# One order list for all steps and loads of an attention and expert kernel: loads of q, k, v and of each weight placed singly, and fillers placed for the clock

## The chip, the cores and the metric

The kernel runs on one core of one Trainium2 chip. The metric is the device time of a run in microseconds (us); a profile shows the span from the first to the last instruction, some 1.6 us less than the time of the same execution. Engines: PE is TensorE (matrix products), PEld its weight loads, DVE is VectorE, ACT is ScalarE, POOL is GpSimd, SP is SyncE. Each works through its own line of instructions in order.

## The reference

Eight batches. Each first passes an attention without softmax, then its 576 x 512 result goes through one of eight experts, picked by the mean of that result.

```python
kv  = einsum('bhsd,bhse->bhde', k, v)            # 8 batches, 8 heads, 576 x 64
out = einsum('bhsd,bhde->bhse', q, kv)
x   = out / rms(out) * g_norm                    # heads side by side: 576 x 512
e_idx = argmax(x.mean(axis=1) @ w_gate)          # one expert per batch
gate  = softmax probability of that expert
result[b] = gate * (relu(x[b] @ w1[e]) @ w2[e])  # 512 -> 1024 -> 512
```

So the expert's weights (2.1 MB as fp16, read as fp32) can only be fetched when the batch's attention is over.

## The kernel before

The whole program is a list of tokens, `ORDER`, which is emitted from left to right into the lines of the engines. `3O1` is batch 3, step O, head pair 1. Steps: T transposes q, K is k times v, O is q times kv, M the mean square, X the normalisation, G0 to G3 the gate (product, expert, power, scale), m0 to m7 the first expert layer and m8 to m16 the second, D a filler product, meant only to keep TensorE's clock up, L a load of q, k, v, W a load of the weights, Q a VectorE copy of q. R, C and P belong to batch 0 alone: R casts its first loads, C evicts its transposes, P copies its gate row and hands PSUM (where TensorE's products lie until an engine evicts them) over to the other batches. A final `x` changes the evicting engine.

```python
def load_qkv(b, parts, which=None):          # one token L: q, k and v together
    ... bufs: qt 3, kt 4, vt 4
    nc.gpsimd.dma_start(t[0:R, hs], src[b, hs]...)

def s_dl(b, mx, pg):                         # part of the gate's value, not of the choice
    ...
    nc.gpsimd.tensor_tensor(lg, base, dl, ALU.pow)     # in GpSimd's line

def s_w(b):                                  # one token W: W1 and W2 together
    ...                                      # VectorE copies an old slot, in case the
    nc.vector.tensor_copy(W[:, own, ...], W[:, ds(sv, 1), ...])   # expert is there
    nc.gpsimd.dma_start(W1[:, own, :, fs], moe_w1[ds(ev, 1), ...], cond=cond)
    nc.gpsimd.dma_start(W2[:, own], moe_w2[ds(ev, 1)]..., cond=cond)
```

Dots mark what is cut, the comments are added. `cond` skips the load when one of the two batches before used the same expert; with these data the weights of batches 1 and 7 are skipped. All these loads cast fp32 to fp16 and are issued by GpSimd, in order, between its power operations and its waits for the expert's number.

Of the kernel before, what the change touches and what calls it, by code (L numbers as in the profile page):

```python
# [16 lines left out]
ALU = mybir.AluOpType  # L17
# [4 lines left out]




ORDER = (
    "0D9 0R1 0R2 0R0 0K02 0T02 0C0 0O0 0K12 0T12 0C1 0M0 0O1 0K22 0T22 0X0 0C2 0M1 0O2 "
    "0K32 0T32 0X1 0C3 0M2 0O30 0O31 0D4 0M30 0M31 0D6 0X2 0X30 0X31 0G1 0P0 1K0 1T0 1O0 "
    "1T1x 1T2 1T3x 1O2 0m0x 1O1 0m3x 1M0 0m5x 1X0 2L0 1M2 1M1 1O3x 1X1 0m7x 1M3 0m6 1X2 "
    "0m1 0G2 1X3 0G3 0m4 1G0 0m2 1G1 0m13 0m15 2Q0 1G3 2T0x 0m14 3L0 2T3x 2T2x 0m16x 0m11 "  # L30
    "0m12x 1W0 2T1 2K0 0m9 2O0 2O1 0m10 2M0 2X0 0m8x 2O2 2O3 3Q0 1m0 2M1 1m3x 2M2 1m7 2X1 "
    "2X2 2M3 2X3 3T0x 1m1 2G0 4L0 3K0 1m5 2G1 3O0x 1m2 3M0 1m6 3T1x 2W0 1m4 3T2 3X0 2G3 "
    "1m11 3T3x 3O1 1m12x 1m15 4Q0 3M1 3O3 1m13 4T0 1m16 3M3 3O2 1m14 1m8x 3X1 5L0 4K0 3M2 "
    "1m9 3X2 3X3 3G0 4T1x 1m10x 4O0x 2m0x 2m4x 4T3x 4T2 2m1 3G1 2m3 2m7 4M0 2m2 4O1x 3W0 "
    "2m6x 4O3x 2m5x 2m13 4M1 3G3 5Q0 2m14x 4X0 5T0x 4X1 2m9 4M3 2m10 4O2 5K0 2m8x 2m15 "
    "5T3 4M2 4X2 4X3 2m16x 5O0x 2m11 2m12 4G0 5T2x 3m0x 6L0 5M0 5O2 5X0 3m6 3m7 5T1 4G1 "
    "3m2 5O1 3m1x 5M2 3m5 6Q0 3m3 5M1 3m4 4W0 3m11 7L0 4G3 6T0x 6T3x 3m12x 6T2x 3m8x 6K0 "
    "5O3 3m15 5X1 3m16x 5X2 5M3 3m13 5X3 3m14 3m9 6O0 3m10x 5G0 4m0 5G1 4m7x 6M0 6O2x "
    "4m4x 6O3x 4m3x 6X0 4m1 6M3 4m5 5G3 6M2 4m2x 6T1x 4m6 5W0 4m11 6O1x 4m9 4m12x 7Q0 6M1 "
    "4m10 4m15 7T0 6X1 7T3x 4m16 7T1x 7K0 6X2 4m8x 7T2 6X3 7O0x 4m13 4m14x 7M0 6G0 5m0x "  # L40
    "7O2x 5m4x 6G1 5m2 7X0 5m7 6W0 5m5 5m1 5m3 5m6x 7M2 7O3 5m11 7O1 5m9 6G3 5m12x 5m10 "
    "7M1 7X1 7X2 7M3 5m13 7X3 5m14x 5m15 5m16 5m8 6m0 7G0 6m1 6m3 6m4x 6m2x 7G1 6m7 6m6 "
    "7G3 6m5 6m9 6m10 6m15 6m16x 6m11 7W0 6m12 6m13 6m14 6m8x 7m0 7m7 7m2 7m5 7m3 7m4 7m1 "
    "7m6 7m9 7m10x 7m13 7m14x 7m15 7m16x 7m11 7m12 7m8x "
)


# [1 line left out]
def kernel(  # L49
# [16 lines left out]
    P = 128  # L66
# [22 lines left out]

    st = [dict() for _ in range(B)]  # L90

    def load_qkv(b, parts, which=None):
        if kvq[b] is None:
            kvq[b] = [pqkv.tile([P, H, NJ, Dh], F16, tag=n, name=n, bufs=nb)
                      for n, nb in (("qt", 3), ("kt", 4), ("vt", 4))]
        step = H // parts
        for i in (range(parts) if which is None else which):
            for t, src in zip(kvq[b], (q, k, v)):
                hs = slice(i * step, (i + 1) * step)
                nc.gpsimd.dma_start(  # L100
                    t[0:R, hs], src[b, hs].rearrange("h (p j) d -> p h (j d)", j=NJ))
# [36 lines left out]
    def psum(tag, bufs=2, nb=2):  # L138
        return psp[0].tile([P, nb, 512], F32, tag=tag, name="ps_" + tag, bufs=bufs)
# [4 lines left out]
    def warm(t, n):  # L144
        for _ in range(n):
            nc.tensor.matmul(t[:, 0, :], ones, kvb[:, 1], start=True, stop=True)  # L146


    def s_qt(b, c, x=False, w=0):
        s = st[b]  # L150
        if "qT" not in s:
            s["qT"] = att.tile([P, NP, S], F16, tag="qT", name="qT")
        p32 = psum("t", 1, 1) if first[0] else psum("a")
        warm(p32, w)
        pt = p32.bitcast(F16)
        for j in range(NJ):
            if "qr" in s:
                nc.tensor.transpose(pt[:, 0, j * R:(j + 1) * R], s["qr"][0:R, c, j],  # L158
                                    ident[0:R, 0:R])
                continue  # L160
            for i in range(2):
                nc.tensor.transpose(pt[64 * i:64 * i + 64, 0, j * R:(j + 1) * R],
                                    kvq[b][0][0:R, 2 * c + i, j, :], ident[0:R, 0:R])
        s["pt", c] = pt
        if b > 0:
            s_tc(b, c, x)
# [12 lines left out]
    def s_tc(b, c, x=False):  # L179
        copy(x, st[b]["qT"][:, c, :], st[b]["pt", c][:, 0, 0:S])  # L180

    def s_kv(b, prs, w=0):
        kt, vt = kvq[b][1:3]
        kv = kvb[:, b % 2]
        p32 = psum("kv", 1, 1) if first[0] else psum("a")
        warm(p32, w)
        pk = p32[:, 0].rearrange("p (c e) -> p c e", c=NP)
        for c in prs:
            for j in range(NJ):
                for i in range(2):  # L190
                    nc.tensor.matmul(pk[64 * i:64 * i + 64, c, 64 * i:64 * i + 64],  # L191
                                     kt[0:R, 2 * c + i, j, :], vt[0:R, 2 * c + i, j, :],
                                     start=(j == 0), stop=(j == NJ - 1))
        cs = slice(prs[0], prs[-1] + 1)
        nc.vector.tensor_copy(kv[0:64, cs, 0:64], pk[0:64, cs, 0:64])
        nc.vector.tensor_copy(kv[64:128, cs, 64:128], pk[64:128, cs, 64:128])
# [52 lines left out]
    def s_row():  # L249
        s = st[0]  # L250
        pg = psum("t", 1, 1)[0:1, 0, 0:E]
        for c in range(NP + 1):
            nc.tensor.matmul(pg, s["pl"][:, c:c + 1], wg[:, min(c, NP - 1)], start=(c == 0),
                             stop=(c == NP))
        s["pg"] = pg
        s_index(0, pg)
        s_w(0)

    def s_index(b, pg):
        n = pg.shape[0]  # L260
# [6 lines left out]
    def s_dl(b, mx, pg):  # L267
        dl = sm.tile([P, E], F32, tag="dl", name="dl")
        nc.vector.tensor_scalar(out=dl, in0=pg, scalar1=mx[:, 0:1], scalar2=None,
                                op0=ALU.subtract)  # L270
        lg = sm.tile([P, E], F32, tag="lg", name="lg")
        nc.gpsimd.tensor_tensor(lg, base, dl, ALU.pow)  # L272
        st[b]["lg"] = lg

    def s_gate2(b):
# [18 lines left out]



    def s_w(b):
        own = b % NW
        cond = None
        if b > 0:  # L300
            sv = 0
            if b > 1:
                sv = nc.vector.value_load(st[b]["src"][0:1, 0:1], min_val=0, max_val=NW - 1)
            for W in (W1, W2):
                for h in range(2):
                    n = W.shape[2] // 2
                    nc.vector.tensor_copy(  # L307
                        W[:, own, h * n:(h + 1) * n],
                        W[:, ds(sv, 1), h * n:(h + 1) * n].rearrange("p o c f -> p (o c) f"))
            for e in evs[max(0, b - 2):b]:  # L310
                c = evs[b] != e
                cond = c if cond is None else s_logical_and(cond, c)
        ev = evs[b]
        nh = {0: 4, B - 1: 2}.get(b, 1)
        for h in range(nh):
            fs = slice(h * F // nh, (h + 1) * F // nh)
            nc.gpsimd.dma_start(W1[:, own, :, fs],  # L317
                                moe_w1[ds(ev, 1), :, fs].rearrange("o (c p) f -> p (o c) f", p=P),
                                cond=cond)
        nc.gpsimd.dma_start(W2[:, own], moe_w2[ds(ev, 1)].rearrange("o (c p) d -> p (o c) d", p=P),  # L320
                            cond=cond)
        st[b]["w"] = (W1[:, own], W2[:, own])

    def s_gate3(b):
        if b == 0:
            pg = psum("a")[:, 0, 0:E]
            nc.tensor.matmul(pg, mean[0:1], st[0]["row"], start=True, stop=True)
            mx = sm.tile([P, 8], F32, tag="mx", name="mx")
            nc.vector.max(mx, pg)
            s_dl(0, mx, pg)  # L330

    def s_gate4(b):
        gs = sm.tile([P, 1], F32, tag="gs", name="gs")
# [4 lines left out]
    def m_1(b, fb, x=False):  # L338
        s = st[b]
        if fb == 0:  # L340
            s["hT"] = hp.tile([P, 8, S], F16, tag="hT", name="hT")
        w1 = s["w"][0]
        ph = psum("m")
        for c in range(4):
            for i in range(2):
# [15 lines left out]

    def m_2(b, t, fcs, x=False):
        s = st[b]
        w2 = s["w"][1]
        if fcs[0] == 0:
            s["pm2", t] = psum("m")
        po = s["pm2", t]
# [46 lines left out]
    def emit(tok):  # L414
        x = tok[-1] == "x"
        b, f, c = int(tok[0]), tok[1], tok[2:].rstrip("x")
        h = None
        if len(c) > 1 and f in "OMXKT":
            c, h = c
            h = int(h)  # L420
        c = int(c or 0)
        if f == "m":
            unit(b, c, x)
        elif f == "D":
            warm(psum("kv", 1, 1), c)
        elif f == "R":
            cast_first(c)
        elif f == "P":
# [4 lines left out]
                                                    space=bass.MemoryType.PSUM))  # L433
            first[0] = False
        elif f == "K":
            s_kv(b, [c] if b == 0 else range(NP), h or 0)
        elif f == "C":
            s_tc(b, c)
        elif f == "G":
            if (b, c) == (0, 1):  # L440
                s_row()
            else:
                (s_gate, s_gate2, s_gate3, s_gate4)[c](b)
        elif f == "Q":
            s_qr(b)
        elif f == "W":
            s_w(b)
        elif f == "L":
            load_qkv(b, 1)
        elif f == "T":  # L450
            s_qt(b, c, x, h or 0)
        elif f == "O":
            s_o(b, c, h, x)
        else:
            dict(M=s_m, X=s_x)[f](b, c, h)
# [33 lines left out]
```

## Time and profile before

| | before |
|---|---|
| time, median of 3 (then 4) runs | 208.54 us (207.93) |
| span of the profiled execution | 203.4 us |
| TensorE busy | 179.3 us, 88% |
| VectorE / ScalarE / GpSimd busy | 116.2 / 103.4 / 51.4 us |
| cast loads / outputs and first loads | 26.30 MB / 10.05 MB |
| first expert product | 29.4 us |
| first product with W1 of batch 5 | 149.19 us |

### The profile page before, as it was taken

To read this page: it belongs to the slowest core of one execution; us is meant where nothing else is said; L and a number is where in the kernel's file an instruction comes from. 1 tells how busy PE (TensorE), PEld (TensorE's weight loads), DVE (VectorE), ACT (ScalarE), POOL (GpSimd) and SP (SyncE) were. 2 spreads that over 40 slices of the span, in tenths; PEclk is the share of its full clock that TensorE was granted. 3 is DMA by queue.
4 is the path that set the end of the run, shared out by engine and by line. 5 is a ranking of instruction groups with operands and counts; after the bars stand their busy time and mean duration, and the time that the engine had idled before them with its cause. 6 is when DMAs were issued, how large, how long until landed. Compare 5 with 4: busy or idle time off the path is not lost.

```text
span 203.4 us, 4406 instructions
## 1 busy us (share of the span) xinstructions
PE 179.3 (88%) x1709; PEld 115.3 (57%) x1709; DVE 116.2 (57%) x292; ACT 103.4 (51%) x165; POOL 51.4 (25%) x64
## 2 busy tenths in 40 slices
PE   6887578979885999998999879999979999999990
PEld 2343356735565656874677534775658558558650
DVE  1446338649693788688564744669836773360010
ACT  2245045724782865686565813775546623316520
POOL 7720390256300750083003160303005100300000
PEclk9999959999999999999999988999999999999998
DMA  6999299998999999999999999999998999053053
GB/s 161 185 202 204 42 146 192 204 203 106 261 234 204 161 182 224 253 211 210 251 237 226 192 170 199 262 214 201 207 259 146 184 179 273 6 149 88 0 147 85
DMA packets 37031, 36.92 MB, mean 182 GB/s; under 512 B 2706, under 2 KB 30354, under 8 KB 37010
## 3 DMA queue, kind: packets, MB, share of 16 engines
q0 software_dynamic: 29328, 26.30, 83.0%
q1 hardware_dynamic: 7474, 10.05, 17.1%
q10 hardware_dynamic: 208, 0.29, 0.5%
q8 instruction: 13, 0.21, 0.4%
q14 instruction: 8, 0.07, 0.1%
HBM read 61.88 MB, written 9.44 MB: 351 GB/s over the span
## 4 chain that ended last, share of the span: by engine, by line
PE 47%; DMA 35%; DVE 6%; POOL 4%; issue 3%; ACT 2%; DVEq 0%; POOLq 0%; ACTq 0%
DMA vt<-in_v_dram 26%; PE ps_m L346 22%; PE ps_m L385 16%; DMA W<-in_moe_w_dram 5%; DMA qt<-in_q_dram 3%; PE ps_a L206 3%; DVE W L307 2%; PE ps_a L223 2%; PE ps_m L373 1%; PE ps_a L191 1%; POOL kt L100 1%; POOL lg L272 1%; ACT sq L211 1%; POOL qt L100 1%; PE ps_a L158 1%
## 5 line engine op out<-in xcount | busy, mean ns | idle before, releaser
L346 PE MATMUL ps_m<-xT,W 128*128 128x288 f16 x512 | 70.2, 288 | 1.8 <-DMA W<-in_moe_w_dram 1.5
L385 PE MATMUL ps_m<-W,hT 128*128 128x512 f16 x256 | 62.3, 386 | 0.0
L346 PEld LDWEIGHTS <-W 128*128 128x128 f16 x512 | 49.8, 99 | 15.6 <-DMA W<-in_moe_w_dram 2.0
L353 ACT ACTIVATE hT<-ps_m 128x576 f16<-128x576 f32 x44 | 28.7, 653 | 22.6 <-PE ps_m L346 22.3
L385 PEld LDWEIGHTS <-hT 128*128 128x128 f16 x256 | 24.8, 99 | 24.6 <-issue 1.5
L272 POOL TENSOR_TENSOR lg<-base,dl 128x8 f32<-128x8 f32 x8 | 14.8, 1849 | 89.2 <-DVE src L291 77.4
L211 ACT ACTIVATE sq<-ps_a 128x576 f16<-128x576 f32 x28 | 18.0, 650 | 18.2 <-PE ps_a L206 18.0
L357 ACT ACTIVATE ot<-ps_m,gates 128x512 f32<-128x512 f32 (+1 forms) x24 | 15.0, 626 | 22.8 <-PE ps_m L385 12.6
L227 ACT ACTIVATE rs<-ps_a,epsc 128x576 f32<-128x576 f32 x28 | 20.5, 740 | 10.0 <-PE ps_a L223 9.7
L236 DVE SCALAR_TENSOR_TENSOR xT<-o,gcol,rs 128x576 f16<-128x576 f32 x28 | 22.2, 811 | 2.5 <-ACT rs L227 2.3
L359 DVE TENSOR_SCALAR ot<-ps_m,gates 128x512 f32<-128x512 f32 (+1 forms) x16 | 11.7, 731 | 19.8 <-PE ps_m L385 19.6
L350 DVE TENSOR_SCALAR hT<-ps_m 128x576 f16<-128x576 f32 x20 | 15.1, 756 | 11.8 <-PE ps_m L346 11.7
L307 DVE COPY W<-W 128x2048 f16 (+1 forms) x28 | 19.5, 719 | 4.1 <-DMA W<-in_moe_w_dram 1.6
L177 DVE COPY o<-ps_a 128x576 f32<-128x576 f32 x17 | 12.7, 756 | 9.4 <-ACT sq L211 9.2
L177 ACT COPY qT<-ps_a 128x576 f16<-128x576 f16 x18 | 11.3, 641 | 9.8 <-PE ps_a L158 8.6
L317 POOL DMA_DIRECT2D W<-in_moe_w_dram x12 | 7.5, 632 | 30.8 <-DVE W L307 13.8
L206 PE MATMUL ps_a<-qT,kvb 128*128 128x288 f16 x56 | 11.6, 296 | 2.1 <-DVE qT L177 1.4
L191 PEld LDWEIGHTS <-kt 96*64 96x64 f16 x384 | 7.3, 114 | 10.7 <-issue 10.5
L191 PE MATMUL ps_a<-vt,kt 96*64 96x64 f16 x336 | 6.6, 196 | 7.5 <-DMA vt<-in_v_dram 7.5
L223 PE MATMUL ps_a<-sq,ones 128*128 128x288 f16 x56 | 11.4, 292 | 0.8 <-DVE o L177 0.8
L146 PE MATMUL ps_kv<-kvb,ones 128*128 128x512 f16 x27 | 9.3, 479 | 2.8 <-DVE ones L128 2.0
L206 PEld LDWEIGHTS <-kvb 128*128 128x128 f16 x64 | 6.1, 100 | 8.0 <-issue 4.0
(76 smaller groups left out, 150.8 us busy)
## 6 DMA issues: line engine op xcount, KB each, us to landing
W<-in_moe_w_dram POOLq DMA_DIRECT2D x14, 1024.0 KB, 12.8
out_dram<-ot SPq DMA_DIRECT2D x24, 192.0 KB, 5.9
qt<-in_q_dram POOLq DMA_DIRECT2D x7, 576.0 KB, 18.6
kt<-in_k_dram POOLq DMA_DIRECT2D x7, 576.0 KB, 15.8
vt<-in_v_dram POOLq DMA_DIRECT2D x7, 576.0 KB, 19.4
out_dram<-ot SPq DMA_DIRECT2D x40, 64.0 KB, 5.7
out_dram<-ot SPq DMA_DIRECT2D x16, 128.0 KB, 6.3
W<-in_moe_w_dram POOLq DMA_DIRECT2D x4, 256.0 KB, 5.7
```

What stands on the lines that cost most here:

```text
L177: nc.scalar.copy(out, in_) if x else nc.vector.tensor_copy(out, in_)
L191: nc.tensor.matmul(pk[64 * i:64 * i + 64, c, 64 * i:64 * i + 64], kt[0:R, 2 * c + i, j, :], vt[0:R, 2 * c + i, j, :], start=(j == 0), stop ...
L206: nc.tensor.matmul(po[:, i, 0:HS], kvb[:, b % 2, c, :], s["qT"][:, c, i * HS:(i + 1) * HS], start=True, stop=True)
L211: nc.scalar.activation(part(s["sq", c], h), po, AF.Square)
L223: nc.tensor.matmul(pm[:, i if h is None else 0, 0:HS], ones, s["sq", c][:, i * HS:(i + 1) * HS], start=True, stop=True)
L227: nc.scalar.activation(part(s["rs", c], h), pm[:, 0:2 if h is None else 1, 0:HS], AF.Abs_reciprocal_sqrt, bias=epsc)
L236: nc.vector.scalar_tensor_tensor(out=part(s["xT"][:, c, :], h), in0=s["o", c, h], scalar=gcol, in1=part(s["rs", c], h), op0=ALU.mult, op1= ...
L272: nc.gpsimd.tensor_tensor(lg, base, dl, ALU.pow)
L307: nc.vector.tensor_copy(W[:, own, h * n:(h + 1) * n], W[:, ds(sv, 1), h * n:(h + 1) * n].rearrange("p o c f -> p (o c) f"))
L346: nc.tensor.matmul(ph[:, i, 0:HS], w1[:, c, fb * P:(fb + 1) * P], s["xT"][:, c, i * HS:(i + 1) * HS], start=(c == 0), stop=(c == 3))
L353: nc.scalar.activation(two(s["hT"][:, fb, :]), ph[:, :, 0:HS], AF.Relu)
L385: nc.tensor.matmul(po[:, 0, :], s["hT"][:, fc, t * P:(t + 1) * P], w2[:, fc, :], start=(fc == 0), stop=(fc == 7))
```

## The change

Its intent: search the order of all steps and of every single load together, with TensorE's clock in the model of the search. L takes q, k or v singly, W takes W1 or W2 singly, the power operation becomes a token of its own (G2), q gets a fourth buffer, and batch 1's first transposes may use batch 0's PSUM tiles. The same products are computed; 35 fillers become 17.

```diff
-    "0D9 0R1 0R2 0R0 0K02 0T02 0C0 0O0 0K12 0T12 0C1 0M0 0O1 0K22 0T22 0X0 0C2 0M1 0O2 "
-    "0K32 0T32 0X1 0C3 0M2 0O30 0O31 0D4 0M30 0M31 0D6 0X2 0X30 0X31 0G1 0P0 1K0 1T0 1O0 "
-    "1T1x 1T2 1T3x 1O2 0m0x 1O1 0m3x 1M0 0m5x 1X0 2L0 1M2 1M1 1O3x 1X1 0m7x 1M3 0m6 1X2 "
-    "0m1 0G2 1X3 0G3 0m4 1G0 0m2 1G1 0m13 0m15 2Q0 1G3 2T0x 0m14 3L0 2T3x 2T2x 0m16x 0m11 "
...
+    "0R1 0R2 0R0x 0K0x 0T0 0C0 0K1 0T1x 0O0x 2L0x 0C1 0D1 0O1x 0M0x 0K2x 0X0 0T2 0M1 0C2x "
+    "0D1 0D1 0O2x 0T3 0X1x 0C3 0K3 0M2x 1T0 0O30x 0O31 0M30 2L2x 0D1 0D1 0D1 0X2 0M31 0D1 "
+    "0X30 0D1 0D1 0X31x 0G1x 0W0x 2L1x 0P0x 0D1 1T1 1T2 1T3 0D1 0D1 0D1 0D1 0D1 0W1 0D1 "
+    "2Q0x 0D1 0G2x 1K0 2T0x 1O0 1O2 1M0 0G3 0m0 2T2 1O1 0m3x 3L0x 3L1 1M1 1X0x 1O3 0m4 "
...
-    def load_qkv(b, parts, which=None):
+    def load_qkv(b, parts, which=None, only=range(3)):
-                      for n, nb in (("qt", 3), ("kt", 4), ("vt", 4))]
+                      for n, nb in (("qt", 4), ("kt", 4), ("vt", 4))]
...
+    def s_pow(b):
         lg = sm.tile([P, E], F32, tag="lg", name="lg")
-        nc.gpsimd.tensor_tensor(lg, base, dl, ALU.pow)
+        nc.gpsimd.tensor_tensor(lg, base, st[b]["dl"], ALU.pow)
...
-    def s_w(b):
+    def s_w(b, i):
+        W = (W1, W2)[i]
```

## The prediction

> **What bounds the kernel now.** I read the slices of the span first, then the chain of waits, then the transfers issued by GpSimd in order of time, and last the busy time in stretches of 5 us and of 1 us. TensorE has the highest share (88%), but the slices say where it is not the bound:
>
> ```profile
> PE   6887578979885999998999879999979999999990
> ...
> PEclk9999959999999999999999988999999999999998
> DMA  6999299998999999999999999999998999053053
> ```
>
> The DMA row stands at 9 nearly without a break up to slice 31 (about 158 us), and after that has little to do; TensorE has dips (slices 5, 9, 13, 24) until then and none afterwards, until the tail. So there are two stages: transfers pace the first, TensorE the second. The chain, in order of time, finds the boundary:
>
> ```profile
> 11.05 12.11 DMA vt<-in_v_dram
> ...
> 47.71 15.29 DMA vt<-in_v_dram
> ...
> 92.66 25.62 DMA vt<-in_v_dram
> ...
> 138.59 10.55 DMA W<-in_moe_w_dram
> 149.15 0.05 issue
> 149.19 1.16 PE ps_m L346 x8
> ```
>
> (Start, length, what.) Three long pieces are loads of v, whose landing lets the next attention start; the last transfer on the chain is W1 of batch 5, landed at 149.15 us. From there to 198.66 us the chain is TensorE alone (49.5 us at full clock, busy 5.00 of every 5 us to 195), then 4.7 us of eviction and output. Thus the end is 149.15 + 49.5 + 4.7 = 203.4 us, and a change is worth what it takes off the 149.15, plus what it alters in the last 54.
>
> In that first stage the loads are late because the queue ran dry, not only because it is slow. In stretches of 5 us (TensorE, weight load, VectorE, ScalarE, GpSimd busy, clock, DMA share, GB/s):
>
> ```profile
> 15.00:20.00 5.00, 3.76 (x38) 1.59 (x37) 2.82 (x8) 2.99 (x6) 0.00 (x0) 1.00 1.32 204
> 20.00:25.00 5.00, 2.99 (x76) 1.87 (x75) 1.77 (x10) 0.00 (x1) 1.17 (x2) 0.95 0.36 57
> 25.00:30.00 5.00, 3.52 (x43) 2.57 (x44) 1.81 (x4) 2.27 (x4) 5.00 (x7) 0.50 1.10 131
> ...
> 45.00:50.00 5.00, 5.00 (x83) 3.09 (x81) 4.22 (x9) 2.97 (x5) 3.63 (x6) 1.00 0.89 111
> ...
> 115.00:120.00 5.00, 2.80 (x75) 2.15 (x72) 2.04 (x6) 1.88 (x5) 3.83 (x5) 1.00 0.99 154
> ```
>
> A saturated stretch has a share of 1.31 to 1.32 and lands 204 GB/s as fp16 (twice that read, since the loads cast from fp32). Against 1.31, rows of 1 us give four holes: 21 to 26 us has 1.01 in five rows, so (6.55 - 1.01)/1.31 = 4.2 us; 46 to 51 us has 4.41, so 1.6; 69 to 72 us has 2.59, so 1.0; 116 to 119 us has 2.55, so 1.05. Together about 8 us; the 5-us rows, which also catch thin places between, give about 11 before 149 us. The GpSimd rows say why:
>
> ```profile
> 11.05 0.77 POOL L100 DMA_DIRECT2D vt<-in_v_dram  x1 [0.32 <-DMA qt<-in_q_dram]
> 23.83 3.00 POOL L317 DMA_DIRECT2D W<-in_moe_w_dram  x4 [12.01 <-issue]
> ...
> 39.45 2.18 POOL L272 TENSOR_TENSOR lg<-base,dl 128x8 f32<-128x8 f32 x1 [9.42 <-DVE dl L269]
> 43.99 1.72 POOL L272 TENSOR_TENSOR lg<-base,dl 128x8 f32<-128x8 f32 x1 [2.36 <-DVE qr L172]
> 45.66 0.82 POOL L100 DMA_DIRECT2D qt<-in_q_dram  x1
> ```
>
> GpSimd issues in order. After batch 1's loads it waits for the expert of batch 0 (issue at 23.83) while the data is through at 21.4; later batch 3's loads stand behind two power operations and go out at 45.66, when the queue is empty at 46.
>
> **What the Trainium skill says.** "DMA: Bandwidth & Descriptors", "Anatomy of one DMA", puts about 2 us of fixed time on a transfer, mostly the receipt of the last write. The trace agrees: data thins at 21.4 us and the wait on v ends at 23.30. So a load must be issued well before the queue empties. The same page, "Issuing engines are not separate DMA queues", says everything shares the 16 engines; the trace agrees in that outputs and loads together reach 258 GB/s and no engine's loads run beside a full queue for free. "TensorE: Matmul & The Clock Gate", Part 1, has a half clock after about 3.4 us idle and a full one after as much work. The trace shows 0.50 from 25 to 31 us and from 120 to 123 us, after idle gaps of only 1.5 and 2.2 us: the two levels agree, the needed gap is shorter here.
>
> **The change, part by part.**
> 1. Loads. q and v of batch 2 go out before batch 0's expert is known. Each lands 0.59 MB; two take 1.18/0.204 = 5.8 us, so data flows from 21.4 to 27.2 and the 4.2 us hole closes. W1 of batch 0 then starts 27.2 rather than 25.5: about 1.7 us later. K of batch 2 goes between W1 and W2 (2.9 us more for W2: data ends at 27.2 + 5.1 + 2.9 + 5.1 = 40.3, landing 42, about when its first matmul comes, before at 42.65).
> 2. Batch 3's q and k are issued right after the first power operation and before the wait for batch 1's expert: with the gate early in the order, about 32 us rather than 45.66. The 1.6 us hole closes. qt gets a fourth buffer, so q of later batches waits for nobody. Loads of 5 go before the weights of 2, and from batch 3 on q, k, v and W1, W2 alternate; W of batch 4 is issued after 2 of batch 3's first-layer units instead of 8, so some 6 units x 0.98 = 6 us earlier in TensorE's work. Holes three and four should close.
> 3. Bytes are the same: 26.30 MB cast loads, 9.44 MB out.
> 4. TensorE work: the same matmuls, except fillers, 35 before and 17 after. None is before the first k-v product now, and one or two in each head pair in place of four (in the trace two take 0.53 to 0.60 us and stand in TensorE's line). A head pair is 2.6 to 2.9 us now, of which about 1.1 us filler. Its own matmuls, about 1.2 us, would take up to 2.4 at half clock: near zero net. Eight fillers and three transposes of batch 1 fill the wait at 22 us and keep the clock.
> 5. Evictions: ScalarE takes 7 more relu (0.653 us), 5 more 512-wide scalings (0.626), and 3 fewer each of narrow scalings (about 0.4), o copies and qT copies (0.64): 4.6 + 3.1 - 1.2 - 3.8 = +2.7 us of 103; VectorE loses about as much of 116. Neither binds.
>
> The sum: of 8 to 11 us of holes I take 7 as removed, since an order searched on modelled times will leave some. W1 of batch 5 is then in at 142. TensorE must be there too: from 23.30 to 149.19 is 125.9 us, less 13 us idle and about 4 lost at half clock: 109 us of work. From about 28 us this gives 137, with some small waits 140. So both meet near 142. Then 49.5 + 0.5 (a transpose and a product of batch 7 slip behind) + 4.7: 196.7 us of span, 0.967 of 203.4. On the 208.54 us median: 201.6.
>
> **The rivals.**
> First, the transfers are already saturated and the order only permutes them: nothing moves, 207 to 209. For it: the 9s, and the 25.62 us landing, which is a backlog. Against: the four holes, each with an issue that came late.
> Second, the start gives it back. VectorE is in order and must now copy q of batch 2 (4 x 0.35 us, landing near 26) before the casts of batch 1's kv, which it did at 24.28; they come at about 27.5. With a cold array and W1 later by 1.7 us, the first expert matmul could move from 29.4 to 32 or 33. If nothing absorbs that: 204. I count on the transfers, ahead by then, absorbing it.
> Third, TensorE or waits on evictions become the bound before batch 5, as the denser stage leaves VectorE (up to 4.6 of 5 us in the row of 55 to 60 us) no slack: 203 to 205.
> Fourth, all 11 us and the half-clock stretches are recovered: a span of 192, 197 us.
>
> **Range and chances.** The step from 142 is firm, the arrival at 142 has an uncertainty of about 4 us either way, and runs of the kernel before differ by 3.3 us. So 196.5 to 206.5. Over 2% faster means under 204.4, which needs only 4 of the 8 to 11 us: 0.78. Within 2%: 0.20. Slower needs two rivals together: 0.02.
>
> **What would show it.** Right: a DMA share near 1.3 from 20 to 25 and 45 to 50 us; batch 3's q issued before 36 us; the first matmul with W1 of batch 5 at 139 to 145 us; TensorE alone for about 50 us after it. Wrong: this matmul near 149 in spite of a full queue, or new TensorE gaps of over 2 us waiting for VectorE or ScalarE; or a first expert matmul after 33 us followed by no catching up.

## The result and the profile after

The time is 195.58 us in the median (193.51 to 197.72, 4 runs) against 207.93 of before. The ratio of the fast runs is 0.9352, with a 95% interval of 0.923 to 0.947. A ratio here is the mean time of one kernel's fast runs over that of the other's of the same rounds, so it is not quite the ratio of the medians. The range (196.5 to 206.5) was missed at its lower end; the direction was right.

The profiled execution after has a span of 191.9 us. The slices (tenths busy, TensorE's granted clock, DMA):

```profile
PE   0296687998999999999999999999999999999990
PEclk9999997999999999999999999999999999999999
DMA  5999999999999999999999999999999898162044
```

TensorE's row stays at 9 after slice 10 until the tail, and the DMA row has no break before slice 31. The stretches of 5 us in which the gaps were (columns: TensorE, weight load, VectorE, ScalarE, GpSimd busy, clock, DMA share, GB/s):

```profile
20.00:25.00 5.00, 3.40 (x52) 1.60 (x51) 2.11 (x9) 0.50 (x1) 0.70 (x1) 1.00 1.32 203
...
45.00:50.00 5.00, 4.61 (x37) 2.48 (x35) 4.45 (x12) 4.13 (x8) 3.55 (x5) 1.00 1.32 204
...
115.00:120.00 5.00, 5.00 (x38) 3.21 (x37) 2.67 (x9) 3.09 (x5) 0.34 (x1) 1.00 1.24 244
```

The shares of 0.36, 0.89 and 0.99 have become 1.32, 1.32 and 1.24. GpSimd's rows show how (start, length, instruction, in brackets the idle time before and its releaser):

```profile
12.37 0.77 POOL L103 DMA_DIRECT2D vt<-in_v_dram  x1
24.30 3.01 POOL L322 DMA_DIRECT2D W<-in_moe_w_dram  x4 [11.16 <-DVE qT L179]
...
28.98 1.68 POOL L275 TENSOR_TENSOR lg<-base,dl 128x8 f32<-128x8 f32 x1
30.63 0.81 POOL L103 DMA_DIRECT2D qt<-in_q_dram  x1
```

Batch 2's q and v are issued by 12.4 us, before the expert of batch 0 is known. The first power operation runs at 28.98 us (before: 39.45), so batch 3's q goes out at 30.63 us (before: 45.66). The chain of waits ends its transfer part 11.7 us earlier:

```profile
127.33 10.08 DMA W<-in_moe_w_dram
137.41 0.05 issue
137.46 3.12 PE ps_m L348 x24
```

The first product with W1 of batch 5 starts at 137.46 us. From there TensorE alone needs until 187.49 us, that is 50.0 us, and 4.4 us of eviction and output follow. In the whole profile the products of both expert layers wait only 0.2 us for a weight (in the second layer), so TensorE and the transfers arrive together.

### The profile page after: what moved, and what is told of

Same layout as the page of the kernel before. It is cut to its first block, busy times and chain, and to the rows that moved or that the text cites. A ratio compares the mean times of both kernels' runs of the same rounds, so it can differ in the third digit from the quotient of the medians.

```text
span 191.9 us, 4365 instructions
## 1 busy us (share of the span) xinstructions
PE 172.1 (90%) x1691; PEld 113.8 (59%) x1691; DVE 111.2 (58%) x289; ACT 106.6 (56%) x168; POOL 49.9 (26%) x64
## 3 DMA queue, kind: packets, MB, share of 16 engines
q0 software_dynamic: 29328, 26.30, 86.4%
HBM read 61.88 MB, written 9.44 MB: 372 GB/s over the span
## 4 chain that ended last, share of the span: by engine, by line
PE 71%; DMA 16%; DVE 5%; ACT 3%; issue 2%; POOL 2%; POOLq 0%
PE ps_m L348 32%; PE ps_m L387 25%; DMA qt<-in_q_dram 7%; DMA W<-in_moe_w_dram 5%; PE ps_a L224 4%; DMA kt<-in_k_dram 4%; PE ps_a L207 3%; PE ps_a L160 3%; PE ps_m L375 3%; DVE o L179 2%; ACT sq L212 2%; PE ps_a L192 2%; DVE qr L174 1%; POOL qt L103 1%; DVE W L311 1%
## 5 line engine op out<-in xcount | busy, mean ns | idle before, releaser
L355 ACT ACTIVATE hT<-ps_m 128x576 f16<-128x576 f32 x51 | 33.2, 652 | 21.0 <-PE ps_m L348 20.7
L322 POOL DMA_DIRECT2D W<-in_moe_w_dram x20 | 12.5, 627 | 74.3 <-DVE W L311 23.6
L359 ACT ACTIVATE ot<-ps_m,gates 128x512 f32<-128x512 f32 (+1 forms) x26 | 17.0, 656 | 18.5 <-PE ps_m L387 12.2
L179 DVE COPY o<-ps_a 128x576 f32<-128x576 f32 x20 | 15.0, 757 | 14.0 <-ACT sq L212 13.8
L361 DVE TENSOR_SCALAR ot<-ps_m,gates 128x512 f32<-128x512 f32 (+1 forms) x14 | 9.4, 674 | 17.8 <-PE ps_m L387 15.9
L179 ACT COPY qT<-ps_a 128x576 f16<-128x576 f16 x15 | 9.5, 636 | 10.7 <-PE ps_a L160 10.7
L352 DVE TENSOR_SCALAR hT<-ps_m 128x576 f16<-128x576 f32 x13 | 9.8, 755 | 8.1 <-PE ps_m L348 8.1
L224 PEld LDWEIGHTS <-ones 128*128 128x128 f16 x64 | 6.0, 99 | 7.9 <-issue 3.2
L160 PEld LDWEIGHTS <-qr 96*128 96x128 f16 x144 | 8.9, 100 | 2.9 <-issue 0.4
L160 PE MATMUL ps_a<-ident,qr 96*128 96x96 f16 x144 | 10.4, 209 | 0.2 <-DVE dl L269 0.2
```

Of the source, the lines that this page charges most:

```text
L160: nc.tensor.transpose(pt[:, 0, j * R:(j + 1) * R], s["qr"][0:R, c, j], ident[0:R, 0:R])
L179: nc.scalar.copy(out, in_) if x else nc.vector.tensor_copy(out, in_)
L224: nc.tensor.matmul(pm[:, i if h is None else 0, 0:HS], ones, s["sq", c][:, i * HS:(i + 1) * HS], start=True, stop=True)
L355: nc.scalar.activation(two(s["hT"][:, fb, :]), ph[:, :, 0:HS], AF.Relu)
L359: nc.scalar.activation(out, in_, AF.Copy, scale=gates[:, b:b + 1])
```

## The experiments

All runs are on one core, each beside runs of the kernel before on its own chip. Names with b_ start from the kernel before, with a_ from the kernel after. The fences under the names give each edit in short, as tokens and places, not as whole diff lines; the b_ kernels with single loads use the code of the kernel after. Two effects have to be kept apart from the edits. First, the time of any one kernel spreads, mostly along with the mean clock of the run: the kernel after took 193.5 to 194.9 us in eight fast runs, whose mean clocks were 0.98 to 1.00, but 196.5 to 199.4 us in five slow runs, most at 0.95 to 0.97, and once 201.81 at 0.983. Second, some profiles fell into a slow run; this is said where it matters. The intervals of b_early2, b_all_w, b_pow3, b_loads2 and b_all exclude equal times, but not a difference under 2%; the record's verdict on each is "unclear".

### Loads alone

**b_early2**: batch 2's loads moved ahead of batch 0's expert, nothing else.

```diff
- ... 0m5x 1X0 2L0 1M2 ...
- ... 0X30 0X31 0G1 0P0 ...
+ ... 0m5x 1X0 1M2 ...
+ ... 0X30 0X31 2L0 0G1 0P0 ...
```

> The kernel before with batch 2's three loads alone moved ahead of the wait for batch 0's expert. If each gap of the queue counts by itself, the 4.2 us gap at 21 to 26 us closes and the span falls by 3 to 4 us (199 to 200, ratio about 0.98). If the queue is only as full as what has been issued, the same bytes are queued by 45 us and the gap comes back at 41 to 47 us, larger by what was saved: span within 1.5 us of before, ratio 0.99 to 1.01, and batch 0's first expert product 3 to 5 us later.

Measured: 212.68 us, ratio 1.0311 (1.017 to 1.045): slower. The gap closed at 21 to 26 us and came back, as the second view had it. Busy times by 5 us in its profile (a slow run):

```profile
40.00:45.00 5.00, 4.51 (x36) 3.48 (x36) 3.78 (x11) 4.22 (x7) 0.04 (x1) 1.00 0.12 19
45.00:50.00 5.00, 3.55 (x25) 2.08 (x24) 2.84 (x14) 1.30 (x2) 2.63 (x2) 1.00 0.01 3
```

The share of 0.12 and 0.01 is an empty queue for about 10 us, more than expected. The three loads also delay batch 0's weights, so the first expert product comes at 33.0 us instead of 29.4; the power operation behind the expert units comes at 44.96 instead of 39.45 (part of this is the slow run: the clock row reads about 0.5 from 25 to 38 us, in the kernel before from 25 to 31); and batch 3's q, behind that, goes out at 51.16 instead of 45.66. A gap cannot be filled by itself: what fills it delays the step that lets the next load go. That the time would stay within 1.5 us was a miss.

**b_loads**: the old steps with the loads of q, k, v about where the kernel after has them (in the code of the kernel after, four q buffers). Batch 3's loads were still behind the power operation in its old place.

```diff
+ 2L0 2L2 before 0G1, 2L1 between 0W0 and 0W1, 3L0 3L1 3L2 behind 0G2,
+ 5L0 5L2 5L1 before 3K0, 6L0 6L1 behind 2W1, 6L2 behind 3W0,
+ 7L0 before 4W0, 7L1 behind it, 7L2 behind 4W1
```

> The steps of the kernel before, in their old order, with only the loads of q, k and v issued at about the places of the kernel after (and four q buffers). Theory A, the order of the transfers made the gain: at least 7 of the 11.5 us of span come, so a span of 192 to 197 us and a ratio to before of 0.945 to 0.967, no gap in the DMA share from 20 to 50 us. Theory B, the new order of the steps on TensorE made it: 200 to 204 us, ratio 0.985 to 1.0, though the gaps in the DMA share are gone.

Measured: 206.26 us, ratio 1.0045 (0.994 to 1.015): nothing gained. But it did not test what it was meant to: batch 3's q left at 42.90 us and the DMA share from 40 to 45 us was 0.64, so a gap stayed.

**b_pow3**: three moves together, the power operation among them.

```diff
+ 2L0 2L2 before 0G1, 2L1 behind 0W0, 0G2 before 1K0, 3L0 3L1 3L2 behind 0G2
```

> The kernel before with its old steps and three moves together: batch 2's q and v issued before the wait for batch 0's expert, the first gate power operation put ahead of batch 1's k-v product instead of behind the first expert units, and batch 3's loads right behind it (about 31 us in place of 45.7). Theory C, the loads are gated by steps in GpSimd's line and these three moves free them: no gap in the DMA share up to 50 us, the 2.9 us wait for batch 3's v at 60 us gone, W1 of batch 5 some 5 to 7 us earlier, span 196 to 199, ratio to before 0.965 to 0.98. Theory B, only the whole new order of steps helps: span 201 or more, ratio over 0.985.

Measured: 205.18 us, ratio 0.9798 (0.972 to 0.988). The ratio is at the edge of what theory C gave; the spans of the fast runs, 202.0 and 205.0 us, are theory B's. Its profile fell into a slow run (span 205.4). In it the 2.9 us wait for batch 3's v is gone, but gaps stand at 25 to 30 us (DMA share 0.60, as in b_all below) and at 65 to 75 us (0.58 and 0.79): the queue is drained earlier and the next weights are issued no earlier (69.68 us, 68.96 before).

**b_loads2**: as b_pow3, with batch 4's loads and the q of 5, 6 and 7 earlier.

```diff
+ 4L0 4L1 4L2 behind 1G2, 5L0 before 2W0, 6L0 before 3W0, 7L0 before 4W0
```

> As b_pow3, and batch 4's loads right behind batch 1's power operation, and the q of batches 5, 6 and 7 one weight load earlier, each where the kernel after has it. Theory C: the gaps at 69 to 72 and 116 to 119 us shrink too, 1 to 3 us more than b_pow3: span 194 to 197, ratio 0.95 to 0.965. Theory B: no better than b_pow3 within 1 us.

Measured: 204.89 us, ratio 0.9795 (0.974 to 0.985): the same as b_pow3, as theory B has it. In its profile (a slow run) the new q of batch 5 left only at 72.01 us, behind the power operation of batch 2, so this place for it was badly chosen. The shares of 0.28 from 30 to 35 us and 0.25 from 70 to 75 us show that its queue was not full either.

**b_all** was meant as the fair form: every load where no gap should be left, the steps in their old order.

```diff
+ b_pow3, and 5L0 5L2 5L1 before 3K0, 6L0 6L1 behind 2W1, 6L2 behind 3W0,
+ 7L0 before 4G1, 7L1 behind 4W0, 7L2 behind 4W1
```

> The steps of the kernel before, with all loads placed without a gap in mind: batch 2's q and v before batch 0's expert, the first power operation early and batch 3's loads behind it, batch 5's behind batch 4's, batches 6 and 7 between the weights of 2, 3 and 4. Theory A, full queue is enough: no gap over 1 us in the DMA share up to 130 us, span of a run at clock 0.97 or more of 193 to 197, ratio to before 0.94 to 0.96. Theory B, the steps must be reordered too, because they decide when weights can be issued: W of batches 2 to 4 still issued at about 69, 89 and 116 us, ratio 0.965 to 0.985.

Measured: 204.88 us, ratio 0.9809 (0.973 to 0.989), fast runs of 202.65 and 203.70 us. Theory B's range. The issues of W1 of batches 3, 4 and 5 in the kernel before, in the kernel after and in b_all (slow run):

```profile
88.79 0.99 POOL L317 DMA_DIRECT2D W<-in_moe_w_dram  x1 [0.60 <-DVE W L307]
...
115.98 0.81 POOL L317 DMA_DIRECT2D W<-in_moe_w_dram  x1 [5.92 <-DVE W L307]
...
138.59 0.99 POOL L317 DMA_DIRECT2D W<-in_moe_w_dram  x1 [7.05 <-DVE W L307]
```

```profile
87.36 0.76 POOL L322 DMA_DIRECT2D W<-in_moe_w_dram  x1 [3.08 <-DVE W L311]
...
102.04 0.76 POOL L322 DMA_DIRECT2D W<-in_moe_w_dram  x1 [1.11 <-PE ps_m L348]
...
127.33 0.80 POOL L322 DMA_DIRECT2D W<-in_moe_w_dram  x1 [2.58 <-PE ps_a L224]
```

```profile
93.75 0.81 POOL L320 DMA_DIRECT2D W<-in_moe_w_dram  x1 [0.26 <-DVE W L309]
...
117.80 0.81 POOL L320 DMA_DIRECT2D W<-in_moe_w_dram  x1 [3.72 <-DVE W L309]
...
139.07 0.81 POOL L320 DMA_DIRECT2D W<-in_moe_w_dram  x1 [7.05 <-DVE W L309]
```

To take out the different starts, count from the first expert product (29.4, 30.8 and 34.2 us) to the issue of W1 of batch 5: 109.2 us before, 96.5 after, 104.9 in b_all. So these places of the loads gave some 4 us, and the kernel after 8 more. This split is an estimate from one profile each, that of b_all in a slow run.

The queue of that profile was not full, so theory A's condition was not met:

```profile
25.00:30.00 5.00, 3.90 (x75) 2.72 (x73) 1.70 (x8) 0.00 (x0) 1.57 (x3) 0.50 0.57 88
...
115.00:120.00 5.00, 5.00 (x57) 3.65 (x56) 3.23 (x8) 3.97 (x7) 2.19 (x3) 1.00 0.45 60
```

The first gap goes with the slow run (b_loads, a fast run with the same early loads of batch 2, has a share of 1.19 there): the clock reads 0.50 from 21 us on, six fillers take 2.72 us (1.46 in the kernel before), and the weights of batch 0 go out at 28.43 us in place of 23.83. The second is theory B's: the weights of batch 4 left only at 117.80 us. Some loads, those of batch 4 among them, also stand later than in the kernel after (53.58 against 45.39 us), so the 8 us need not be the steps' alone. The old steps with a queue that is full throughout were not run.

**b_all_w**: b_all with the weights of 3, 4 and 5 right behind their expert's decision.

```diff
+ 3W0 6L2 3W1 behind 3G2, 4W0 7L1 4W1 7L2 behind 4G2, 5W0 5W1 behind 5G2
```

> As b_all, and the weights of batches 3, 4 and 5 directly behind their expert's decision instead of some units later. Theory A: 1 to 2 us better than b_all. Theory B: the copies between weight slots then sit earlier in VectorE's line and delay evictions: no better than b_all within 1 us.

Measured: 212.14 us, ratio 1.0242 (1.014 to 1.035): 4% worse than b_all. The mechanism of theory B shows in the longest of TensorE's waits (total, times, longest), in a fast run:

```profile
PE ps_m L346 <- DVE hT L350: 6.7, 2, 4.9
```

VectorE stands at the copies between weight slots, and an eviction of the first layer waits behind them. W alone, moved to these places, lost as well.

### Undoing parts of the kernel after

**a_late2**: batch 2's loads behind batch 0's weights again.

```diff
+ 2L0x 2L1x 2L2x behind 0W1; 2Q0x 2T0x 2T2 behind 1G0
```

> The kernel after with batch 2's q, k and v issued behind both weights of batch 0 (its q copy and its first transposes moved behind the first expert units so that VectorE is not blocked). Theory A: a gap of about 4 us at 21 to 26 us returns, W1 of batch 5 lands 3 to 5 us later, span 194.5 to 197, ratio to before 0.95 to 0.97. Theory B: TensorE has other work, span within 1.5 us of 191.9, ratio 0.93 to 0.945.

Measured: 204.18 us, ratio 0.9927 (0.984 to 1.001), span 202.1: nearly all the gain is lost. The 4 us gap is back (DMA share 0.33 from 20 to 25 us), but it cost 10 us. The chain shows why: batch 2's v was issued at 29.86 and landed 19.14 us later, at 49.0; the product of batch 2's k and v stands in TensorE's line before the gate of batch 1; so batch 1's power operation came at 52.49 us in place of 43.76, and W1 of batch 5 was issued at 136.40 in place of 127.33. Batch 2's late loads had moved every later issue of weights by about 9 us. (The clock row reads half from 24 to 37 us here, against 31 to 34 in the kernel after; the chain up to 49.0 us goes through the load all the same.) Theory A's direction held, its size was half of what came.

**a_late3**: batch 3's loads behind batch 1's power operation.

```diff
+ 3L0x 3L1 3L2x 4L0x 4L1 behind 1G3x; 3Q0 before 3T0x
```

> The kernel after with batch 3's loads issued behind the power operation of batch 1 as in the kernel before (about 45 us in place of 30.6), and batch 4's behind them. Theory A: the queue empties at 40 us, a gap of about 6 us, W1 of batch 5 lands 4 to 7 us later, span 196 to 199, ratio to before 0.96 to 0.975. Theory B: within 1.5 us of 191.9, ratio 0.93 to 0.945.

Measured: 205.50 us over six runs (200.8 to 206.64), ratio 1.0001 (0.990 to 1.011). This ratio overstates the loss: it is the mean of 204.97, 206.02 and 206.64 us, three runs (clocks of 0.95 to 0.97). Two runs (200.80 and 203.22 us) make 0.981 of the fast runs of before, close to theory A's range, and the profiled run, the fastest, has a span of 199.1, at the top of it. In that profile:

```profile
40.00:45.00 5.00, 4.55 (x74) 3.49 (x69) 3.29 (x11) 3.31 (x7) 1.95 (x2) 1.00 0.38 63
...
55.00:60.00 5.00, 1.50 (x50) 1.47 (x51) 0.00 (x0) 0.23 (x1) 0.78 (x1) 0.64 1.25 245
```

The queue is empty from 40 us (share 0.38), and 15 us later TensorE, VectorE and ScalarE stand idle together for batch 3's v (4.1 us of TensorE's time). W1 of batch 5 was issued at 134.37 us, 7.0 later than in the kernel after, and the span is 7.2 us longer.

**a_group67**: the loads of 6 and 7 behind both weights, not between them.

```diff
+ 6L0x 6L1x 6L2x behind 3W1; 7L0x 7L1 7L2x behind 4W1x
```

> The kernel after with the loads of batches 6 and 7 not interleaved with W1 and W2 of batches 3 and 4 but all behind them, as in the kernel before. If the interleaving matters: the q of batch 6 lands late and VectorE, in order, waits with it, span longer by 3 us or more, ratio to before over 0.95. If by then the queue is far enough ahead: within 1 us, ratio 0.93 to 0.94.

Measured: 220.79 us, ratio 1.0556 (1.045 to 1.066), much slower than both. The first line of TensorE's waits:

```profile
PE ps_a L160 <- DVE qr L174: 20.4, 2, 10.8
```

Twice, for 10 us each, VectorE stood at the copy of a q that had not landed, and everything behind it in its line stood too. Only the loads were moved, the copies 6Q0 and 7Q0 stayed. The steps of the new list are laid out for these loads; with the loads at the old kind of place the same steps are worse than the old kernel.

### Without the bytes

**b_quarter** and **a_quarter**: from batch 1 on only a quarter of each weight is fetched. Every instruction stays. Their outputs are wrong, which doesn't matter for the times.

```diff
-  W[:, own, :, fs]   <- moe_w[ev, :, fs]
+  W[:, own, 0:q4, fs] <- moe_w[ev, 0:q4*P, fs]     # q4 = a quarter, batch 0 whole
```

> The kernel before with a quarter of the bytes of every expert weight load from batch 1 on (wrong result on purpose; every instruction stays). Theory A, transfers pace it until 149 us: the waits of TensorE for v and W (7.5 and 3.5 us) and the half clock after them go, span 188 to 194 us, ratio 0.92 to 0.95. Theory B, the order of steps on TensorE paces it: 199 us or more, ratio 0.98 or more.

Measured: 200.51 us, ratio 0.9591 (0.953 to 0.965). Between the theories. Fewer bytes take 4% off the kernel before, yet it stays slower than the kernel after with all its bytes. Its wait of 2.9 us for batch 3's v is still there, because batch 3's loads are still issued at 46 us. A late issue is not mended by fewer bytes in the queue.

> The kernel after with the same quarter weights (wrong result on purpose). If TensorE and the transfers now meet, as the profile has it (0.2 us of waits for W), the span falls by at most 2 us: 190 to 192, ratio to before 0.92 to 0.935. If the transfers still pace it: 186 us or less, ratio under 0.91.

Measured: 195.13 us, ratio 0.9333 (0.927 to 0.940), the same as the kernel after in full (span 192.8 us, just above the 190 to 192 expected). A hit in the ratio: the bytes of the weights no longer set the time.

### Fillers and the clock

**a_nofill**: all 17 D tokens removed.

```diff
- 0D1 (17 times)
```

> The kernel after without its 17 filler products. If they keep the clock up through the wait at 22 to 26 us: half clock from about 25 us on, span longer by 1 to 3 us (193 to 195, ratio to before 0.94 to 0.955). If they only cost time in line: shorter by up to 1 us (191 to 192, ratio 0.93 to 0.935).

Measured: 195.84 us, ratio 0.9368 (0.932 to 0.942), span 194.2. In this profile the clock row shows full speed from the start, but 12 k-v products take 0.53 us at 6 and still at 17 us (0.36 us at 15.7 us in the kernel after), and the first expert product comes at 32.9 us in place of 30.8. So the array ran at half speed until about 36 us, and the fillers are worth 1 to 2 us in the profiles (194.2 against 191.9, 192.9 and 193.2 us in three of the kernel after); the timed ratios (0.9368 against 0.930 to 0.938) do not separate the two.

**a_fill9**: the nine start fillers put back; **a_fill9b** is the same file beside the unchanged kernel.

```diff
+ "0D9 " at the head of the list
```

> The kernel after with the nine fillers of the kernel before put back at the very start, where TensorE only waits for the first load. They heat the clock before the first products, which now run at half clock: the products of the first two pairs fall from 0.53 and 0.70 us to 0.3 and 0.45, but those pairs wait for loads, so the argmax of batch 0 comes at most 0.5 us earlier and the span is within 0.7 us of 191.9 (ratio 0.93 to 0.938). If the cold start costs more: 1.5 to 3 us shorter.

> The nine start fillers put back in the kernel after, now beside it on one chip. If a warm start is worth something: 0.5 to 1.5% below a_again2 in fast runs. If not, and the lower ratio of the first run was the draw of the clock: within 0.5%.

Measured: 194.83 us, ratio 0.9247 (0.918 to 0.931) in the first; 197.59 us, ratio 0.9513 (0.945 to 0.958) in the second. The first looked 0.6% better than the kernel after on the same chip (a_again), the second 1.4% worse (a_again2). Its mean clock was 0.93 to 0.96 in the second and up to 0.98 in the first, while a_again2's fast runs had 0.99 to 1.00, so the second does not compare like with like. The start fillers bring nothing that can be relied on, and no version here beats the kernel after reliably.

**a_again**, **a_again2**: the kernel after, unchanged.

> The kernel after unchanged, to compare with the others of this call on the same chip and to see how its time goes with the granted clock from run to run: ratio 0.925 to 0.945, and [...]times that fall by 2 us or more as the mean clock rises from 0.96 to 0.99.

> The kernel after unchanged: ratio 0.925 to 0.945 to before; fast runs 193.5 to 195 us at a mean clock of 0.98 or more, slow ones 196 to 199.5 us at 0.95 to 0.97.

Measured: 194.57 us, ratio 0.9302 (0.924 to 0.936), and 196.32 us, ratio 0.9377 (0.929 to 0.946). As expected, save for the one run of 201.81 us at a clock of 0.983, which the mean clock does not explain.

## Why the prediction was wrong in size

**What bounds the kernel** was right as far as it went: the arrival of W1 of batch 5, then TensorE alone. The last two terms of the sum held: 50.0 us (predicted 49.5 + 0.5) and 4.4 us (4.7).

**The term that failed** is "Together about 8 us; the 5-us rows ... give about 11", of which "I take 7 as removed", and with it the arrival at 142 us. It was 137.46, so the time gained was 11.7 us and not 7. That is 4.7 us of the 4.8 us by which the span of 191.9 fell below the predicted 196.7. The conversion to time (the ratio of spans on the median) was good: the spans give 0.9435, the medians 0.9406.

It was not the filling of the holes that was misjudged. Measured in the prediction's own way (rows of 1 us with a DMA share under 1.0, set against 1.31), the holes up to this product come to 7.4 us before and 0.6 us after (8.9 us in the profile of b_all): about 7 us removed, as it took. What failed is the step from holes to time. On TensorE's side, from 23.3 us to the first product with W1 of batch 5, the busy time went from 112.7 to 110.5 us and the idle time from 13.2 to 3.7 us, which together is the 11.7. The prediction let its 109 us of work begin at "about 28 us" and added 3 us of waits. In the profile 4.2 us of work (fillers among it) is done between 23.3 and 28 us; after 28 us TensorE is busy for 106.3 us and idle for 3.2, most of it before 50 us. So the waits came, the work from 28 us on was overstated by 2.7 us, and "From about 28 us this gives 137" came out near by two errors that cancel.

**What was wrong behind it** is the picture. The prediction saw two bounds side by side, a queue with gaps in it and TensorE's work, and let them "meet near 142". The runs show a loop instead: a load lands, a step of TensorE's line can go on, a gate behind it chooses the expert, GpSimd issues the next load (the chain of a_late2). A gap is a symptom of where the loop was late. Filling one alone lost (b_early2, +3.1%), taking one batch's loads out of their place costs far more than their gap (a_late2: 4 us of gap, 10 us of span), and W1 of batch 5 lands some 10 us after its issue in the kernels before and after (10.55 and 10.08 us). The issue moved by 11.3 us, from 138.59 to 127.33, and the arrival with it.

**The loads (parts 1 and 2).** Right: the 5.8 us of data fill the first gap (share 1.32), batch 3's q goes out at 30.63 us (about 32 predicted), the weights of batch 4 at 102.04 in place of 115.98 us. That was 14 us, where "some 6 units", 6 us, had been counted, so even here the earlier decision was undervalued. Not borne out: that the loads are the cause by themselves. b_all keeps the old steps (save the power operation) and gains 1.9%, the kernel after 6 to 7%; but b_all's queue still had gaps.

**Bytes (part 3)** were right: 26.30 MB in both profiles.

**Fillers (part 4).** "Near zero net" for batch 0's attention held: its row of experts is ready at about 22 us in both. The fillers in the wait did not quite "keep the clock": the row shows 0.66 from 30 to 35 us.

**Evictions (part 5)**: ScalarE went from 103.4 to 106.6 us (+2.7 predicted, +3.2 measured), VectorE from 116.2 to 111.2 (5.0 less, where about 2.7 had been predicted); neither bound.

**The rivals.** The first (only a permutation) is refuted. The second was real but small: the first expert product came at 30.8 us, 1.5 us later than before, and was absorbed as hoped. The third did not occur in the kernel after, but b_all_w and a_group67 show what it looks like. The fourth, with a span of 192, has the number that came; it was given too little weight. Its mechanism came in part: the holes are filled, but the clock still reads 0.50 from 31 to 34 us. That the 11 us of the 5-us rows lie near the 11.7 gained is in part luck, since the holes removed do not add up to it. The range rested on "an uncertainty of about 4 us either way", and its lower end lay at about 192 us of span (196.5 us in time), which is where the result fell, just outside.

**What was read into the traces.** The row of 258 GB/s (outputs and loads together) does not test whether the queues share the engines: its DMA share is 1.18, below the 1.31 of loads alone. No run here tests it.

**Still open.** Which of the reordered steps, or of the changed evicting engines, bring the 8 us that b_all does not bring was not taken apart, and the old steps with a full queue were not run; that they let the weights of batches 4 and 5 be issued 14 and 11 us earlier is shown, that this is the whole of it is argued. Also open is what decides the clock of a single run.

## What to carry to other kernels

When loads are issued by an in-order engine and depend on decisions that earlier loads feed, gaps in the queue are not separate items to be added up. Follow the loop from landing to step to decision to issue, and compare the issue time of the last critical load, not the fill of the queue. Move loads and the steps that use them together: moves of this kind made alone gave from -2% to +3% here, and undone alone they cost 5% to 13% (fast runs).

## What the Trainium skill lacked or had wrong

- "TensorE: Matmul & The Clock Gate" puts the loss of full clock after about 3.4 us idle. Here 0.50 was recorded from 25 to 31 us and from 120 to 123 us after idle gaps of 1.5 and 2.2 us. In b_all it was recorded from 21 us on with no single gap over 0.6 us in the 8 us before.
- The same page warns that clock events in a trace can be unreliable; it does not say that a profile's clock can read full while the products run at half speed. In a_nofill the mean clock reads 1.00, while 12 k-v products take 0.53 us at 6 us and at 17 us, against 0.36 us when warm.
- No page says how far single executions of one kernel lie apart. The unchanged kernel after took 193.5 to 199.4 us with mean clocks from 1.00 to 0.95 (and once 201.81 us at 0.983), some 3%. That the clock causes it is not shown: one slow run, 196.53 us, had 1.00.
- "DMA: Bandwidth & Descriptors", Specifications, gives about 358 GB/s as the limit of HBM per core; its section on bandwidth says that this is for two cores streaming at once, and has 425 GB/s for one alone. No page has a rate for loads that cast. Here they landed 204 GB/s as fp16, which is 408 GB/s read as fp32.
- No page says that the profile counts skipped conditional loads as read. The page of this kernel says 61.88 MB; all q, k and v (28.3 MB) and eight weight pairs (8 x 4.19 MB) make 61.9, but two of the eight were skipped (issues of 0.04 us in the trace).
